# Attention and gated MLP in one kernel: fewer warming products, the softmax constant and the gate in other instructions, a new step order

## The chip, the cores and the metric

One core of a Trainium2 chip runs the whole program. The metric is device time in microseconds (us); the runs of the kernel before have a median of 676.97 us (three runs, 676.08 to 677.22). Less is better. The engines are named as in the profile: PE is TensorE (PEld its weight loads), DVE is VectorE, ACT is ScalarE, POOL is GpSimd, SP is the queue that issues the transfers.

## The reference

Two computations follow each other. The first is causal attention over 4 batches, 8 heads, 576 positions and 64 features, mixed by a gate per head with a retrieval from a memory matrix:

```python
a = np.exp(scores - scores.max(-1, keepdims=True))
a /= a.sum(-1, keepdims=True) + 1e-09
local = np.matmul(a, v)
g = 1.0 / (1.0 + np.exp(-beta))[None, :, None, None]
x = g * mem_out + (1 - g) * local
```

The second takes x as 2304 tokens of 512 features and computes ((x @ w_a) * (x @ w_b)) @ w_out with 1536 hidden features. The inputs k and z_prev are drawn eight times as wide as the others. Weights come as 64-bit floats, all else as 32-bit.

## The kernel before, in words

Work is cut into 16 **pairs** of heads (4 batches of 4 pairs). For each pair, steps with short names do this: `TK`, `TQ`, `Tq` transpose k, q and the last 64 rows on TensorE; `th*` and `tl*` split the results into a high and a low part (ScalarE and VectorE); `b_*` and `S_*` compute the mask and the scores, three products for each because of the split; `m*` takes the row minimum of the negated scores (line 574); `e*` is the exponential on ScalarE (line 585), which also writes each row's sum; `r_` makes the row factor on VectorE (lines 593 and 596); `n0` to `n4` multiply the five tiles of P by it on GpSimd (line 604), nine instructions for a pair, one for each row tile of 128 and head, with 128 to 512 columns, and one with 576 for the last rows of both heads; `G*` transposes P, `h*` and `l*` split that again, and `V*` multiplies by v (line 704), which `v_h` and `v_l` have split on GpSimd. `st_` stores the result to memory. `L*`, `D*` and `E*` are loads on SP's queue. Between these stand the memory retrieval (`ma` to `py`), the conversion of the MLP's weights (`mag` to `lo`), and from about 200 us on the MLP itself (lines 909 to 956), whose columns fill the rest of the time on TensorE.

The order is written out by hand. `HEAD` names every step for the first pairs. `LOOP` has two lists, each run through once for every loop position, with a lag behind each name that says how many pairs it runs behind; `SPAN` gives positions 3 to 8 to the first list and 9 to 13 to the second. `TAIL` names every step for the last pairs and the start of the MLP. `schedule` (line 114) yields the steps, and every engine takes its own instructions strictly in that order. `BANKS` gives each step that writes PSUM its bank.

In the row factor, the tile `sum` holds nine sums for each of 128 partitions. The step adds 1e-9 and multiplies by `over_ungate`, which is 1 + exp(beta), and so 1 over the share (1 - g), in one instruction, then takes the reciprocal:

```python
nc.vector.scalar_tensor_tensor(
    out=r, in0=r, scalar=1e-9, in1=over_ungate[:, j, :], op0=ALU.add, op1=ALU.mult
)
nc.vector.reciprocal(out=r, in_=r)
```

The scaling takes that factor as its first per-partition operand and the constant 1.0 as its second. `gates` (line 720) fills `over_ungate` once. `warm` (line 383) issues products of a tile of zeros on TensorE, whose results nobody reads: 17 and 12 of them, next to each other, at the very start while the first loads are on their way. `zi` (line 750) fills that tile with zeros.

Of the kernel before, what the change touches and what calls it, by code (L numbers as in the profile page):

```python
# [1283 lines left out]
```

## Time and profile before

| what | us |
|---|---|
| median of the runs | 676.97 |
| the profiled execution | 676.11 |
| its span, first to last instruction | 674.3 |
| TensorE busy in it | 660.1 |
| VectorE busy | 440.0 |
| ScalarE busy | 317.2 |
| GpSimd busy | 236.8 |

Busy time is counted over the whole span, though the first 206 us hold the attention, in which four engines work at once, and the rest the MLP, in which TensorE works almost alone. The busy time of TensorE contains each product's way through the array, so short waits between products don't show in it. A chain of waits is followed back from the last instruction to what released each one. A timeline row with a count merges instructions that follow one another.

### The profile page before, as it was taken

Reading aid. Unit: us, or ns where it says so; the run is one execution under the profiler, and the core shown is the slowest. Engines: PE = TensorE matmul, PEld = TensorE weight load, DVE = VectorE, ACT = ScalarE, POOL = GpSimd, SP = SyncE. Lnnn points to the kernel's source line nnn. Section 1 sums busy time; section 2 is a strip of 40 time slices with the busy share of each in tenths; the row PEclk is TensorE's granted clock in tenths of the full one; section 3 lists DMA queues with packets and bytes.
Section 4 is the critical chain, followed back from the end, with each engine's and each line's share of the span. In section 5 each row is a group of like instructions: output and inputs, shape, how many; then the busy total and the mean of one; then the engine's idle time right before and its main releaser. Section 6 shows DMA issues by size and latency. Waiting matters only on the chain.

```text
span 674.3 us, 11381 instructions
## 1 busy us (share of the span) xinstructions
PE 660.1 (98%) x4125; PEld 609.8 (90%) x4125; DVE 440.0 (65%) x901; ACT 317.2 (47%) x765; POOL 236.8 (35%) x354
## 2 busy tenths in 40 slices
...
GB/s 171 194 179 167 158 97 197 112 180 143 255 152 96 225 150 162 170 112 71 41 104 122 13 59 39 1 90 36 29 36 6 112 36 1 0 48 1 0 1 47
DMA packets 124663, 64.24 MB, mean 95 GB/s; under 512 B 97856, under 2 KB 116288, under 8 KB 124608
## 3 DMA queue, kind: packets, MB, share of 16 engines
...
q14 instruction: 23, 0.19, 0.1%
...
## 4 chain that ended last, share of the span: by engine, by line
PE 79%; DVE 15%; POOL 3%; ACT 2%; issue 1%; ACTq 0%; DVEq 0%; POOLq 0%
PE pp L909 43%; PE o L946 22%; DVE nm L574 4%; PE pt L187 4%; DVE PT L191 4%; PE pw L704 4%; PE pt L535 3%; POOL P L604 1%; PE m L1108 1%; DVE f L191 1%; PE pw L535 1%; PE pt L387 1%; DVE f L193 1%; DVE sum L593 1%; PE pt L909 1%
## 5 line engine op out<-in xcount | busy, mean ns | idle before, releaser
L909 PE MATMUL pp<-xh,wh 128*128 128x384 f32 x568 | 191.5, 337 | 1.8 <-ACT x L921 0.9
L909 PE MATMUL pp<-xh,wl 128*128 128x384 f32 x568 | 191.1, 336 | 0.0
L909 PE MATMUL pp<-xl,wh 128*128 128x384 f32 x568 | 190.4, 335 | 0.0
L924 DVE TENSOR_TENSOR x<-pp,x 128x384 f32<-128x384 f32 x71 | 39.4, 555 | 132.9 <-ACT x L921 121.7
L909 PEld LDWEIGHTS pp<-xh,wh 128*128 128x128 f32 x568 | 106.7, 188 | 5.7 <-ACT x L921 1.6
L909 PEld LDWEIGHTS pp<-xl,wh 128*128 128x128 f32 x568 | 106.7, 188 | 2.9
L909 PEld LDWEIGHTS pp<-xh,wl 128*128 128x128 f32 x568 | 106.6, 188 | 0.0
L921 ACT ACTIVATE x<-pp 128x384 f32<-128x384 f32 x71 | 34.6, 488 | 149.3 <-PE pp L909 134.4
L1100 POOL TENSOR_TENSOR xx<-xx 128x384 f32<-128x384 f32 x16 | 16.7, 1049 | 199.1 <-DMA xx<-xs 198.9
L946 PE MATMUL o<-wh,hl 128*128 128x512 f32 x216 | 85.5, 396 | 0.0
L946 PE MATMUL o<-wl,hh 128*128 128x512 f32 x216 | 85.0, 393 | 0.0
L946 PE MATMUL o<-wh,hh 128*128 128x512 f32 x216 | 84.9, 393 | 0.0
L604 POOL TENSOR_SCALAR P<-P,sum 128x128 f32<-128x128 f32 (+3 forms) x144 | 81.4, 585 | 7.0 <-DVE sum L596 7.0
L585 ACT ACTIVATE P<-pt,nm 128x128 f32<-128x128 f32 (+3 forms) x128 | 67.1, 532 | 11.3 <-DVE nm L574 10.2
L191 DVE TENSOR_TENSOR PT<-pt,PT 128x512 fp32r<-128x512 f32 (+2 forms) x112 | 61.7, 587 | 9.0 <-ACT PT L659 6.7
L704 PE MATMUL pw<-PT,vh 128*128 128x320 f32 (+4 forms) x416 | 62.0, 293 | 3.0 <-POOL P L604 1.1
L704 PEld LDWEIGHTS pw<-PT,vh 128*128 128x128 f32 x416 | 57.3, 189 | 6.0 <-POOL PT L191 1.6
L928 ACT ACTIVATE hh<-x 128x384 fp32r<-128x384 f32 x72 | 37.6, 523 | 50.7 <-DVE x L924 42.1
L191 DVE TENSOR_TENSOR hl<-x,hh 128x384 fp32r<-128x384 f32 x71 | 42.0, 591 | 27.8 <-ACT hh L928 27.6
L574 DVE TENSOR_REDUCE nm<-pt 128x1 f32<-128x128 f32 (+3 forms) x128 | 55.6, 479 | 5.3 <-PE pt L535 5.0
L187 PE MATMUL pt<-ident,P 128*128 128x128 f32 (+1 forms) x400 | 52.3, 276 | 2.0 <-POOL P L604 0.9
L659 ACT ACTIVATE PT<-pt 128x512 fp32r<-128x512 f32 (+2 forms) x112 | 52.1, 527 | 2.6 <-PE pw L704 2.0
...
## 6 DMA issues: line engine op xcount, KB each, us to landing
...
```

What stands on the lines that cost most here:

```text
L187: nc.tensor.transpose(out, x, ident[0:x.shape[0], 0:x.shape[0]])
L191: eng.tensor_tensor(out=lo, in0=x, in1=hi, op=ALU.subtract)
L574: nc.vector.tensor_reduce(out=s["nm"][:, c:c + 1], in_=src, axis=AX.X, op=ALU.min)
L585: nc.scalar.activation(out=s["P", i][:, h, :], in_=src, func=AF.Exp, scale=-1.0, bias=s["nm"][:, c:c + 1], accum_out=s["sum"][:, c:c + 1],)
L604: nc.gpsimd.tensor_scalar(out=pr[:, h, :], in0=pr[:, h, :], scalar1=r[:, c:c + 1], scalar2=1.0, op0=ALU.mult, op1=ALU.mult,)
L659: nc.scalar.activation(out=dst, in_=src, func=AF.Copy)
L704: nc.tensor.matmul(pv[:, a:hi], lhsT=w, rhs=x, start=(n == 0), stop=(n == len(ops) - 1))
L909: nc.tensor.matmul(pp, lhsT=w[:, w0:w0 + P], rhs=x[:, kk, :], start=(c == 0), stop=(c == 3 * KK - 1),)
L921: nc.scalar.activation(out=x, in_=ps[1], func=AF.Copy)
L924: nc.vector.tensor_tensor(out=h[0], in0=ps[0], in1=h[0], op=ALU.mult)
L928: nc.scalar.activation(out=h[1], in_=h[0], func=AF.Copy)
L946: nc.tensor.matmul(po[t, m], lhsT=hx[:, m * P:(m + 1) * P], rhs=w[:, w0:w0 + DM], start=(f == 0 and n == 0), stop=(f == NFT - 1 and n == 2),)
```

## The change

The single call of the warming step asks for 14 products where two calls asked for 17 and 12. The row sums get a tile of their own, two of them in turn: each sum is the first of a pair of columns whose second holds 1e-9, filled once in `zi`. `r_` adds up the pairs with one reduction and takes the reciprocal, without the gate. `gates` takes a reciprocal more, so that `ungate` holds (1 - g), and the scaling on GpSimd multiplies by it as its second per-partition operand. All four lists of steps and banks are new; the steps themselves, their engines and their number are the same but for the warming. The lists of `BANKS` and `TAIL` are left out here.

```diff
--- before.py
+++ after.py
@@ -19,95 +19,95 @@
 
 
 HEAD = """
-Dk.0 id.0 zi.0 ib.0 wm.17 wm.12 TK.0 Dq.0 Dk.1 TQ.0 zq.0 zq.1 thK.0 thQ.0 mk.0 Ek.1 TK.1 thK.1 b_2.0
-tlK.0 tlQ.0 S_2.0 m2A.0 Eq.0 e2A.0 b_3.0 Ek.0 S_3.0 tlK.1 m3A.0 sq.0 Dq.1 Lv.0 Tq.0 be.0 thq.0 Tq.1
-tlq.0 S_4.0 Lk.2 thq.1 m2B.0 tlq.1 TQ.1 e3A.0 e2B.0 b_.0 Lt.2 Lt.3 b_2.1 thQ.1 m3B.0 S_.0 m4.0 tlQ.1
-e3B.0 ms.0 mA.0 Lv.1 e4.0 mB.0 S_2.1 b_3.1 S_3.1 m2B.1 S_4.1 ga.0 m3A.1 eA.0 eB.0 v_h.0 TK.2 r_.0
-e2B.1 b_.1 Lk.3 v_l.0 e3A.1 thK.2 m2A.1 e2A.1 m3B.1 tlK.2 S_.1 ma.2 n0.0 mB.1 Tq.2 n4.0 thq.2 n1.0
-G0.0 n2.0 mb.2 G1.0 e3B.1 tlq.2 G5.0 G4.0 Lk.4 h0.0 TQ.2 h1.0 w_0.0 eB.1 thQ.2 G2B.0 mu.2 m4.1 h5.0
-l1.0 h4.0 G2A.0 n3.0 l0.0 h2B.0 G3B.0 mA.1 l5.0 eA.1 tlQ.2 l2B.0 l4.0 h2A.0 Lv.2 l2A.0 v_h.1 h3B.0
-l3B.0 G3A.0
+id.0 Dk.0 zi.0 ib.0 Dq.0 wm.14 TK.0 mk.0 Dk.1 Dq.1 Ek.0 b_2.0 thK.0 TQ.0 zq.0 Eq.0 zq.1 TK.1 thQ.0
+thK.1 tlK.0 tlQ.0 S_2.0 be.0 b_3.0 TQ.1 Ek.1 Lv.0 S_3.0 m2B.0 tlK.1 ms.0 thQ.1 b_.0 m2A.0 m3B.0
+e2B.0 sq.0 S_.0 tlQ.1 e2A.0 Tq.0 Lk.2 m3A.0 Tq.1 e3B.0 thq.0 thq.1 mB.0 tlq.0 e3A.0 mA.0 tlq.1 Lt.2
+ga.0 S_4.0 v_h.0 b_3.1 b_2.1 m4.0 v_l.0 eA.0 Lv.1 S_2.1 S_3.1 b_.1 eB.0 S_.1 m2A.1 TK.2 m3B.1 e4.0
+Lv.2 r_.0 TQ.2 e2A.1 mA.1 n4.0 G4.0 e3B.1 m2B.1 n0.0 S_4.1 eA.1 thK.2 n1.0 thQ.2 ma.2 h4.0 G0.0 Lk.3
+mB.1 n2.0 eB.1 m3A.1 G5.0 e2B.1 h0.0 G2B.0 G2A.0 tlK.2 Tq.2 G1.0 tlQ.2 h5.0 mb.2 m4.1 v_h.1 h2B.0
+n3.0 G3B.0 l4.0 h2A.0 w_0.0 thq.2 l0.0 mu.2 h1.0 l2B.0 l5.0 G3A.0 l2A.0 e3A.1 tlq.2 h3B.0 l1.0 Lt.3
+Lk.4 l3B.0
 """
 BANKS = """
...
 """
 LOOP = """
-H1:2 hh:4 pd:2 pe:3 shift1:3 TQ:0 py:4 h3A:3 me:3 clamp1:3 l3A:3 mx:3 e4:2 LM:2 b_3:1 thQ:0 px:4
-S_3:1 TK:0 cx:3 m3A:1 ma:0 r_:2 lo0:2 H0:3 Lp:1 mc:1 V1A:3 e3A:1 b_:1 V2A:3 Lt:-1 v_l:2 pb:2 thK:0
-tlQ:0 mb:0 pf:3 b_2:1 S_2:1 S_:1 xA:3 m3B:1 tlK:0 high1:3 m2B:1 n2:2 st_:4 n0:2 hl:4 V1B:3 Tq:0
-high2:3 clamp2:3 e3B:1 e2B:1 mA:1 pc:2 m2A:1 hi0:2 shift0:2 n4:2 eA:1 thq:0 md:1 low0:2 V2B:3 mag2:3
-e2A:1 high0:2 tlq:0 G5:2 xB:3 n1:2 mag0:1 G2B:2 h5:2 n3:2 lo1:4 low1:3 mu:0 G2A:2 sm:3 h2B:2 G0:2
-G1:2 mB:1 h0:2 l5:2 v_h:1 S_4:1 h2A:2 Lv:0 w_0:2 sq:-1 hi1:4 l2B:2 l2A:2 pa:1 h1:2 l1:2 shift2:3
-eB:1 m4:1 G4:2 h4:2 low2:3 l0:2 Lk:-2 G3B:2 clamp0:2 l4:2 h3B:2 mag1:2 G3A:2 l3B:2
+clamp0:2 clamp2:3 shift0:2 low2:3 TQ:0 hh:4 h3A:3 lo1:4 e4:2 Lt:-1 b_3:1 me:3 mc:1 ma:0 thQ:0 S_3:1
+l3A:3 clamp1:3 hi1:4 low1:3 pb:2 H1:2 pd:2 m3A:1 TK:0 v_l:2 V1A:3 V2A:3 pf:3 b_:1 b_2:1 Lp:1 LM:2
+r_:2 S_2:1 low0:2 mb:0 e3A:1 S_:1 thK:0 sq:-1 n4:2 V1B:3 tlQ:0 n2:2 m3B:1 Tq:0 xA:3 n0:2 mag0:1
+tlK:0 e3B:1 m2B:1 V2B:3 pe:3 m2A:1 mB:1 high2:3 mA:1 G0:2 e2B:1 md:1 e2A:1 n1:2 thq:0 G5:2 H0:3
+tlq:0 eB:1 lo0:2 shift2:3 mx:3 high0:2 xB:3 h5:2 py:4 n3:2 mu:0 G2A:2 G2B:2 h2A:2 G1:2 v_h:1 Lv:0
+S_4:1 h0:2 l5:2 G4:2 h2B:2 w_0:2 l2A:2 h1:2 hi0:2 eA:1 l2B:2 sm:3 st_:4 shift1:3 l1:2 l0:2 mag2:3
+hl:4 G3B:2 high1:3 m4:1 h4:2 pa:1 pc:2 cx:3 Lk:-2 h3B:2 mag1:2 l4:2 l3B:2 px:4 G3A:2
 /
-mc ma v_l mag0 b_3 Lk mag1 px h3A S_3 mu e4 pe TK l3A TQ V1A mag2 m3A pb pf r_ V2A st_ b_ b_2 shift2
-H0 S_2 pc S_ thK n1 H1 Tq V1B thQ high0 e3A n2 n4 tlQ xA clamp0 V2B G5 m3B high1 mx clamp2 mb G2B
-m2B G2A lo0 py e3B m2A G1 S_4 low1 e2B e2A thq n0 low0 LM mB G0 mA n3 eA xB tlq lo1 Lp tlK h5 l5 h2B
-pd sq l2B v_h me shift0 hi1 cx h2A hi0 G4 h1 eB Lv l2A G3B l1 h4 h0 G3A m4 Lt l4 sm clamp1 hl h3B hh
-w_0 low2 l0 shift1 l3B md high2 pa
+lo1 hh high1 px md v_l sq h3A b_3 me S_3 pe l3A e4 r_ TK TQ pb V1A high0 hi1 n1 V2A b_ b_2 shift1
+m3A thQ S_2 n2 n0 S_ Tq V1B mag0 V2B e3A thK n4 low2 pf pc tlQ xA mag2 G5 m3B G0 low0 mu G2B clamp2
+m2B Lk e3B G2A e2B m2A mc thq n3 G1 S_4 e2A py H0 mA eA xB h5 pd clamp0 v_h tlK h2B mB tlq ma shift0
+l5 low1 shift2 h0 h2A clamp1 w_0 h1 cx l2B G4 eB Lp G3B h4 high2 l2A Lt lo0 hi0 sm LM Lv l1 st_ h3B
+mx pa m4 l4 hl l0 mb mag1 l3B G3A H1
 """
 SPAN = (3, 9, 14)
 TAIL = """
...
 """
 
 
@@ -179,7 +179,8 @@
     ident = const.tile([P, P], F32, name="ident")
 
     over_gate = const.tile([P, H], F32, name="over_gate")
-    over_ungate = const.tile([P, NP, NTL], F32, name="over_ungate")
+    ungate = const.tile([P, NP, NTL], F32, name="ungate")
+    sums = [const.tile([P, NTL, 2], F32, name=f"sums{i}") for i in range(2)]
 
     over_gate_2 = const.tile([P, NP], F32, name="over_gate_2")
 
@@ -576,23 +577,20 @@
 
         @steps(*PARTS)
         def e(s, b, j, part):
-            if "sum" not in s:
-                s["sum"] = p2.tile([P, NTL], F32, tag="sum", name="sum")
+            s["sums"] = sums[j % 2]
             for i, h, c, src in scores(s, part):
                 if ("P", i) not in s:
                     shape = [P, 2 if i < NF else 1, src.shape[1]]
                     s["P", i] = p2.tile(shape, F32, tag=f"P{i}", name=f"P{i}")
                 nc.scalar.activation(
                     out=s["P", i][:, h, :], in_=src, func=AF.Exp, scale=-1.0,
-                    bias=s["nm"][:, c:c + 1], accum_out=s["sum"][:, c:c + 1],
+                    bias=s["nm"][:, c:c + 1], accum_out=s["sums"][:, c, 0:1],
                 )
 
         @steps("")
         def r_(s, b, j, part):
-            r = s["sum"]
-            nc.vector.scalar_tensor_tensor(
-                out=r, in0=r, scalar=1e-9, in1=over_ungate[:, j, :], op0=ALU.add, op1=ALU.mult
-            )
+            r = s["sum"] = p2.tile([P, NTL], F32, tag="sum", name="sum")
+            nc.vector.reduce_sum(out=r, in_=s["sums"], axis=AX.X)
             nc.vector.reciprocal(out=r, in_=r)
 
         @steps(*(str(i) for i in range(NF + 1)))
@@ -602,8 +600,8 @@
             for h in range(pr.shape[1]):
                 c = 2 * i + h
                 nc.gpsimd.tensor_scalar(
-                    out=pr[:, h, :], in0=pr[:, h, :], scalar1=r[:, c:c + 1], scalar2=1.0,
-                    op0=ALU.mult, op1=ALU.mult,
+                    out=pr[:, h, :], in0=pr[:, h, :], scalar1=r[:, c:c + 1],
+                    scalar2=ungate[:, j, c:c + 1], op0=ALU.mult, op1=ALU.mult,
                 )
 
 
@@ -722,13 +720,14 @@
             for t, sign in ((u, 1.0), (over_gate, -1.0)):
                 nc.scalar.activation(out=t, in_=beta_t, func=AF.Exp, scale=sign)
                 nc.vector.tensor_scalar(out=t, in0=t, scalar1=1.0, scalar2=None, op0=ALU.add)
+            nc.vector.reciprocal(out=u, in_=u)
             u2 = u.rearrange("p (j e) -> p j e", e=2)
             for e in range(2):
                 r = slice(64 * e, 64 * e + 64)
                 nc.vector.tensor_copy(
-                    over_ungate[:, :, e:2 * NF:2], u2[:, :, e:e + 1].to_broadcast([P, NP, NF])
-                )
-                nc.vector.tensor_copy(over_ungate[r, :, NTL - 1], u2[r, :, e])
+                    ungate[:, :, e:2 * NF:2], u2[:, :, e:e + 1].to_broadcast([P, NP, NF])
+                )
+                nc.vector.tensor_copy(ungate[r, :, NTL - 1], u2[r, :, e])
 
         beta_t = p1.tile([P, H], F32, name="beta_t")
         mask = p2_e.tile([P, P], BF16, name="mask", bufs=1)
@@ -747,7 +746,10 @@
                 nc.vector.tensor_copy(mask_t[r], mask_f[r, r])
 
         step |= {
-            "zi": lambda _: nc.vector.memset(idle.bitcast(F32), 0.0),
+            "zi": lambda _: (
+                nc.vector.memset(idle.bitcast(F32), 0.0),
+                [nc.vector.memset(t[:, :, 1], 1e-9) for t in sums],
+            ),
             "zq": blank,
             "id": lambda _: make_identity(nc, ident),
             "ib": lambda _: nc.vector.tensor_copy(ident_b, ident),
```

## Rows read from the trace of the kernel before

**Rows 1.** Busy time by stages: us, then PE, PEld, DVE, ACT, POOL; clock, DMA.
```profile
28.00:88.00 60.00, 58.78 (x510) 52.57 (x510) 59.13 (x132) 56.14 (x163) 57.84 (x90) 1.00 0.61 158
...
100.00:155.00 55.00, 55.00 (x491) 50.88 (x489) 47.58 (x106) 50.18 (x150) 51.59 (x86) 1.00 0.65 167
155.00:206.00 51.00, 48.05 (x404) 43.38 (x403) 44.12 (x87) 42.89 (x116) 48.83 (x75) 1.00 0.53 168
206.00:300.00 94.00, 92.68 (x494) 86.77 (x493) 82.38 (x111) 47.19 (x70) 20.74 (x21) 1.00 0.49 164
```

**Rows 2.** Chain of waits by lines: 28 to 100 us, then 155 to 206 us.
```profile
by line: DVE nm L574 26.3%; DVE PT L191 25.7%; PE pt L187 6.0%; DVE f L191 5.8%; DVE ph L272 5.1%; PE pw L704 4.6%; DVE f L193 4.5%; DVE sum L593 4.3%; DVE rn L282 4.2%; PE pt L535 3.8%; DVE ph L269 3.0%; DVE sum L596 1.8%; issue 1.6%; DVE 
...
by line: PE pw L704 12.3%; POOL P L604 12.2%; DVE PT L191 8.8%; POOL vh L191 6.5%; PE pt L187 6.3%; PE pt L535 6.2%; PE pt L909 4.0%; POOL xl L191 3.8%; POOL xx L323 3.8%; issue 3.0%; POOL PT L191 2.9%; DVE wt L880 2.7%; DVE wt L873 2.7%; D
```

**Rows 3.** Timeline, 0 to 26 us: start, us, engine, line, operation, count, idle before.
```profile
1.19 5.64 PE L387 MATMUL pt<-idle 128*128 128x256 f32 x29 [1.19 <-DVE idle L750]
...
6.66 0.60 PE L187 MATMUL pt<-ident,kr 128*128 128x128 f32 x4
...
7.10 0.60 PE L187 MATMUL pt<-ident,qr 128*128 128x128 f32 x4
...
7.93 0.69 DVE L191 TENSOR_TENSOR f<-pt,f 128x512 fp32r<-128x512 f32 x1 [4.63 <-ACT f L511]
```

**Rows 4.** Warming products by stretch: us, PE, PEld, granted clock, DMA share, GB/s.
```profile
3.00:4.00 1.00, 1.00 (x7) 1.00 (x6) 1.00 1.02 230
```

**Rows 5.** First loads of k, then of q: issue (ns, first and last start) and landing.
```profile
L425 SPq DMA_DIRECT2D kr<-in_k_dram x2: 442/467/492, 0.7 to 1.2; - x2
DMA to landing us min/median/max: 2.3/2.6/2.9
...
L425 SPq DMA_DIRECT2D qr<-in_q_dram x2: 499/503/507, 1.8 to 2.3; - x2
DMA to landing us min/median/max: 2.9/2.9/2.9
```

**Rows 6.** Timeline of POOL, 8 to 60 us: three groups of row scalings.
```profile
18.09 4.18 POOL L604 TENSOR_SCALAR P<-P,sum 128x128 f32<-128x128 f32 x7 [3.06 <-DVE sum L596]
...
39.92 4.97 POOL L604 TENSOR_SCALAR P<-P,sum 128x384 f32<-128x384 f32 x9 [0.66 <-DVE sum L596]
...
51.69 4.98 POOL L604 TENSOR_SCALAR P<-P,sum 128x384 f32<-128x384 f32 x9 [0.38 <-DVE sum L596]
```

**Rows 7.** Lines 593 and 596, whole span: ns least, median, most; first and last start.
```profile
L593 DVE SCALAR_TENSOR_TENSOR sum<-sum,over_ungate x16: 158/276/1625, 17.5 to 191.9; 128x9 f32<-128x9 f32 x16
...
L596 DVE RECIPROCAL sum<-sum x16: 215/216/217, 17.7 to 193.1; 128x9 f32<-128x9 f32 x16
```

**Rows 8.** Timelines of VectorE and GpSimd, 60 to 90 us.
```profile
86.22 1.62 DVE L593 SCALAR_TENSOR_TENSOR sum<-sum,over_ungate 128x9 f32<-128x9 f32 x1
...
86.53 1.29 POOL L191 TENSOR_TENSOR vh<-vr,vh 128x512 fp32r<-128x512 f32 x1
```

**Rows 9.** Pieces of the chain, start and us: to 20 us, then 28 to 100.
```profile
9.27 1.55 PE pt L535 x8
...
62.76 0.36 DVE sum L593
...
86.30 1.55 DVE sum L593
```

**Rows 10.** VectorE's groups by form, whole span: count, busy us, mean ns, idle before.
```profile
L574 DVE TENSOR_REDUCE nm<-pt 128x1 f32<-128x512 f32 x32 | 21.7, 680 | 0.2
...
L574 DVE TENSOR_REDUCE nm<-pt 128x1 f32<-128x128 f32 x32 | 8.9, 279 | 1.7 <-PE pt L535 1.6
```

**Rows 11.** GpSimd by form: one operand (111 to 115.9 us), then none (whole span).
```profile
L604 POOL TENSOR_SCALAR P<-P,sum 128x512 f32<-128x512 f32 x2 | 1.4, 688 | 0.0
...
L604 POOL TENSOR_SCALAR P<-P,sum 128x128 f32<-128x128 f32 x2 | 0.7, 367 | 0.0
...
L451 POOL TENSOR_SCALAR qdiag<-qdiag 128x512 f32<-128x512 f32 x4 | 2.5, 615 | 5.1 <-DMA qdiag<-in_q_dram 5.1
...
L476 POOL TENSOR_SCALAR vh<-vt 128x128 fp32r<-128x128 f32 x16 | 4.7, 296 | 0.7 <-DMA vt<-in_v_dram 0.7
```

More of the change, by code (lines that the diff above doesn't have):

```diff
@@ new lines @@
+pe.12 h4.12 G2B.12 l0.12 l3A.12 v_l.13 m3B.14 e3B.14 r_.13 pd.13 V1A.12 h2B.12 Tq.14 l4.12 TQ.15
+pf.12 m3A.14 h3B.12 V2A.12 n0.13 thq.14 b_.14 l3B.12 thQ.15 n2.13 tlq.14 n1.13 st_.11 e3A.14 xA.12
+pa.13 b_2.14 l2B.12 pb.13 tlQ.15 S_.14 S_2.14 TK.15 n3.13 pc.13 mA.14 V1B.12 eA.14 Tq.15 G0.13
+thK.15 m2A.14 n4.13 m2B.14 V2B.12 e2B.14 G3A.13 thq.15 G4.13 tlK.15 v_h.14 G5.13 S_4.14 h0.13 mB.14
+xB.12 Lp.14 pe.13 tlq.15 v_l.14 w_0.13 h3A.13 h5.13 h4.13 l3A.13 l5.13 G2A.13 eB.14 G1.13 m4.14
+e2A.14 h2A.13 pf.13 G3B.13 h1.13 px.12 b_3.15 l0.13 S_3.15 l4.13 pa.14 l2A.13 e4.14 h3B.13 px.13
@@ new lines @@
+l1.13 pb.14 r_.14 m3B.15 G2B.13 V1A.13 pc.14 py.12 h2B.13 e3B.15 V2A.13 xA.13 b_.15 b_2.15 S_.15
+S_2.15 l3B.13 V1B.13 m3A.15 l2B.13 n4.14 mB.15 e3A.15 V2B.13 m2A.15 m2B.15 n3.14 eB.15 G3B.14 e2A.15
+n0.14 e2B.15 G4.14 xB.13 pd.14 h3B.14 n2.14 mA.15 G5.14 S_4.15 l3B.14 eA.15 h5.14 G0.14 n1.14 m4.15
+l5.14 h4.14 v_h.15 v_l.15 l4.14 G1.14 G2A.14 to.0 h0.14 e4.15 G3A.14 h3A.14 w_0.14 l0.14 h1.14
+h2A.14 r_.15 n0.15 l3A.14 l1.14 n2.15 l2A.14 G2B.14 mag0.15 pe.14 h2B.14 V1A.14 V2A.14 clamp0.15
+l2B.14 st_.13 G2A.15 mag1.15 shift0.15 st_.12 n4.15 n1.15 G2B.15 V1B.14 high0.15 V2B.14 G4.15 G5.15
@@ new lines @@
+Khi.3 umx.1 Kshift.4 Klo.3 uA.2 Kload.8 uhh.1 Kload.9 uhl.1 Kmag.5 Kclamp.5 Khigh.4 Klow.4 Kshift.5
+Kload.10 uB.2 ucx.2 umx.2 uA.3 Khi.4 uhh.2 Kmag.6 Klo.4 uhl.2 Khigh.5 uB.3 Kclamp.6 Klow.5 Kshift.6
+Khigh.6 ucx.3 umx.3 uo.2 uA.4 Klow.6 Khi.5 uB.4 uhh.3 uo.1 Klo.5 uA.5 Khi.6 Kmag.7 uhl.3 uB.5 Klo.6
+ucx.4 Kclamp.7 Kmag.8 uo.3 Kshift.7 Kload.11 umx.4 Kclamp.8 Khigh.7 Klow.7 uhh.4 Kshift.8 uhl.4
+Khi.7 uA.6 Khigh.8 Klo.7 uB.6 Kload.13 ucx.5 Kmag.9 Klow.8 umx.5 Khi.8 uhh.5 Kload.12 uo.4 Kclamp.9
@@ new lines @@
+Kload.14 Kshift.9 Klo.8 Khigh.9 Klow.9 Kmag.10 ucx.6 Kload.16 Kclamp.10 uhl.5 Khi.9 Kshift.10 uA.7
+umx.6 uB.7 Klo.9 Kmag.11 uo.5 uA.8 Khigh.10 uhh.6 uhl.6 Klow.10 Kclamp.11 Kshift.11 Khi.10 Klo.10
+Kload.15 ucx.7 umx.7 uB.8 Kmag.12 uhh.7 ucx.8 Khigh.11 Klow.11 uo.6 Kclamp.12 uhl.7 Kshift.12 Khi.11
+Khigh.12 uA.9 Klow.12 Khi.12 Kmag.13 Klo.11 uB.9 umx.8 uhh.8 Kclamp.13 uo.7 uhl.8 Kshift.13 uA.10
+Klo.12 uB.10 Khigh.13 Kmag.14 Klow.13 ucx.9 umx.9 Kclamp.14 uhh.9 uo.8 Khi.13 Kmag.15 Kshift.14
+ucx.10 Khigh.14 Kload.18 uA.11 Klow.14 uhl.9 Klo.13 Khi.14 Kclamp.15 umx.10 Kshift.15 Klo.14 Kmag.16
@@ new lines @@
+Khigh.15 uB.11 Kload.17 uo.9 uhh.10 Klow.15 Kclamp.16 Kshift.16 Kload.20 ucx.11 uA.12 uB.12 uhl.10
+Khigh.16 Kload.22 umx.11 Kload.19 uo.10 uhh.11 uA.13 Kload.21 Klow.16 Khi.15 Khi.16 uhl.11 uB.13
+uo.11 Kmag.17 Kmag.18 Klo.15 Klo.16 ucx.12 uA.14 Kclamp.17 Kshift.17 Kclamp.18 umx.12 Kshift.18
+Khigh.18 uB.14 uhh.12 Klow.18 Khigh.17 Khi.18 uhl.12 Klo.18 ucx.13 Klow.17 Kmag.20 umx.13 Kclamp.20
+uo.12 Kload.23 Khi.17 Kmag.19 Kshift.20 Klo.17 Khigh.20 uhh.13 uhl.13 Kclamp.19 Kshift.19 ucx.14
+Klow.20 umx.14 Khi.20 Khigh.19 Kmag.22 Klow.19 Klo.20 uA.15 uhh.14 uo.13 uB.15 Khi.19 Kmag.21 ucx.15
```

93 lines of the change are left out of this document (32 added, 61 removed).

## The prediction

> **What bounds the kernel now.** I read the busy time by stages first [rows 1], then the chain of waits by lines [rows 2]. From 206 us on TensorE is busy with 1.3 us of gaps in 94: no operation of that stage changes, and what is won or lost before it moves it as a whole. So the first 206 us decide. Up to 28 us the pipeline fills, and the row of warming products is the longest piece of the chain. From 28 to 88 us VectorE is busy 59.13 of 60 us, and the chain is mostly its instructions; GpSimd stands close behind with 57.84. From 100 to 155 us TensorE has no gap, VectorE 7.4 us spare and GpSimd 3.4. From 155 to 206 us the chain passes between TensorE, GpSimd and VectorE, and GpSimd is busy 48.83 of 51. Then I followed the two lines that change, the row-sum step on VectorE and the scaling of P on GpSimd, into the timeline and the chain.
>
> **Warming products.** Today 29 products run from 1.19 us, and the first transposes of k follow them directly at 6.66, those of q at 7.10 [rows 3]. They stand behind the products alone, not behind their data. The products take 5.64 us, 0.19 us from one to the next. [...] The second half of the first k is issued at 1.24 and takes up to 2.9 us: it is in at 4.1, so its transposes can start 2.4 us sooner. The first q, second half issued at 2.3, is in at 5.2: 1.9 us sooner than used now [rows 5]. [...] I take **-1.2 us**. Bounds: 0, if another part of the filling pipeline holds the scores, and -2.4. On SP's queue the second pair's q now goes ahead of the tails of k and q, beta ahead of the second batch's k tail, and the first v some half a microsecond later. GpSimd, which splits that v, idles 3.06 us before 18.09 for the row sums [rows 6], and that covers it; without that cover it would cost its half microsecond.
>
> **Setup.** The two fills with 1e-9 come on VectorE at about 1 us, in the 4.63 us for which it idles before its first use of k [rows 3]: nothing. The reciprocal of the gate sits among the gate steps, ahead of the first row sums, where VectorE is full: **+0.2 us**, by the 216 ns of the other small reciprocal [rows 7].
>
> **Row sums.** Sixteen steps. The old instruction takes 158 ns at the least, 276 in the median, 1625 at the most, on nine columns; the reciprocal behind it always 215 to 217 [rows 7]. So it is not arithmetic. The old step reads two operands in SBUF, and where it is long it ends with a two-input instruction of GpSimd: one runs from 86.53 to 87.82, and the step from 86.22 to 87.84 [rows 8]. In the VectorE stage it is on the chain six times: four times with 0.36 us, as at 62.76, once with 0.09 and once with 1.55 [rows 9], 3.1 us together. The new sum has one input and should be free of this. Reductions of 512 and 128 columns take 680 and 279 ns [rows 10], 1.04 ns a column and 146 ns fixed, so 18 columns take 165 ns, much as the unhindered old step, some 0.1 us on the chain: six make 0.6, and 2.5 us go. GpSimd allows less: its group of nine starts at 39.92 and again at 51.69, of which 0.38 us is waiting for the row sums [rows 6]; 11.77 can shrink to 11.39 at most, plus what the new scaling adds. I take **-2.2 us**. Bounds: 0, if GpSimd sets the pace, and -2.5. From 100 to 155 us TensorE covers the step: nothing. From 155 to 206 us one long wait of about a microsecond may be on the chain, out of what is left of the sixteen; I take **-0.9**, bounds 0 and -1.5.
>
> **Scaling on GpSimd.** 144 instructions get a second per-partition operand where a constant stood. The trace has no such form. It has one operand and none: 688 against 615 ns at 512 columns, 367 against 296 at 128 [rows 11]. The first operand costs 72 ns. The upper bound for the second is the same again, 144 x 72 = 10.4 us of GpSimd; the lower is nothing, if the form that fetches one fetches both. No row excludes either. The nearest row would say 72, but it measures the step from constants to operands, not from one to two, so I take less, 20 ns: 0.18 us for a group of nine. Up to 88 us this is already in the -2.2; from 100 to 155 GpSimd's 3.4 idle us take it in; from 155 to 206, four groups, **+0.7**.
>
> [...]
>
> **New order.** Steps and engines stay, the sequence on each engine changes, its transfers included. TensorE idles 2.95 us from 155 to 206 and 1.3 up to 300 [rows 1], so an order may win some 1.5 us there, and an operand that comes late may lose as much. I take 0, with 1.5 either way.
>
> **Sum.** -1.2 + 0.2 - 2.2 - 0.9 + 0.7 = -3.4 us against the profiled execution's 676.11 (span 674.3): 672.7. The median of the runs, 676.97, lies 0.86 higher: 673.6.
>
> **Rivals.** *First: GpSimd becomes the bound, and it is slower.* With 72 ns a group of nine grows by 0.65 us. In the VectorE stage GpSimd's period becomes 12.04 for 11.77, +1.35 us in five periods, about what the one long stall gives back: 0. From 100 to 155 us its idle 3.4 us lie unevenly before the groups; of five times 0.65 I count a third, +1.1. From 155 to 206, four times 0.65 less some 0.9 of its idle time: +1.7. With -1.2 and +0.2 that is +1.8: 678.8, and up to 681 with a bad order. It decides from about 42 ns on, where 11.39 us and nine times the price reach 11.77. For it: GpSimd is 96% busy, and the first operand has this price. Against: both may come in one fetch.
>
> [...]
>
> *Third: the change frees nothing that matters.* TensorE is busy 58.78 of 60 us in the VectorE stage, so VectorE may win idle time alone; with the start's -1.0 and +0.5 for the order, 676.5.
>
> **How the numbers follow.** Forecast 0.50, first rival 0.27, second 0.10, third 0.13. The likeliest's own range is 671 to 675.5. The range for 8 in 10 leaves about a tenth on either side: 670.5 (start at -2.4, a better order) and 680.0, inside the first rival. A measurement tells about 0.2%, 1.35 us: faster ends at 675.6, slower begins at 678.3. The forecast gives faster 0.46, the same 0.04; the second and third give 0.08, 0.14 and 0.01; the first gives the same 0.05 and slower 0.22. Together faster 0.54, same 0.23, slower 0.23.
>
> **What would show it.** Right: the first transposes of k at 4.2 to 4.5 us, the first scores a microsecond sooner; the sum at 150 to 200 ns with no long ones and hardly on the chain; the scaling at 512 columns below 715 ns; about 11.5 us from group to group in the VectorE stage. Wrong: 512 columns at 750 ns or more and GpSimd without idle time from 28 us on (first rival); early transposes that take double their time (second); a sum without long waits, and yet the TensorE stage at 206 us reached no sooner than the start alone explains (third).

## The result, and the profile after

The changed kernel takes 682.0 us (median of six runs, 681.35 to 683.71) where the kernel before takes 676.49 in the same call: ratio 1.0088, 95% interval 1.0071 to 1.0106. It is 0.9% slower, above the whole predicted range, in the direction of the first rival.

| | before | after |
|---|---|---|
| the profiled execution, us | 676.11 | 683.25 |
| its span | 674.3 | 681.5 |
| TensorE busy | 660.1 | 659.6 |
| VectorE busy | 440.0 | 445.7 |
| ScalarE busy | 317.2 | 317.4 |
| GpSimd busy | 236.8 | 246.3 |

GpSimd has 9.5 us more to do, VectorE 5.7, TensorE no more than before. The busy time by stages, in the columns of [rows 1], with the stretch between the first two stages as a row of its own; the last row is that stretch in the kernel before:

```profile
28.00:88.00 60.00, 57.49 (x496) 50.33 (x495) 59.11 (x127) 53.70 (x157) 59.06 (x86) 1.00 0.62 148
88.00:100.00 12.00, 9.39 (x74) 8.79 (x74) 11.20 (x22) 7.93 (x26) 11.76 (x19) 0.88 0.57 149
100.00:155.00 55.00, 54.73 (x491) 50.66 (x489) 47.38 (x104) 49.53 (x142) 51.79 (x83) 0.99 0.60 149
155.00:206.00 51.00, 46.41 (x394) 41.38 (x392) 41.17 (x86) 41.92 (x120) 49.08 (x73) 1.00 0.63 191
206.00:300.00 94.00, 91.19 (x495) 86.14 (x495) 79.03 (x107) 47.67 (x73) 25.17 (x27) 0.98 0.42 138
...
88.00:100.00 12.00, 11.31 (x103) 10.49 (x103) 11.57 (x27) 10.55 (x33) 10.62 (x20) 1.00 0.52 117
```

In the VectorE stage GpSimd is now as full as VectorE, 59.06 and 59.11 of 60 us, and TensorE does 496 products there instead of 510. From 88 to 100 us TensorE idles 2.6 us, for 0.7 before, and its granted clock averages 0.88, for 1.00. The chain of waits by lines, from 28 to 100 us, 100 to 155 and 155 to 206, names the engine that the end now waits for; the last line is the kernel before, from 100 to 155 us:

```profile
by line: DVE nm L575 29.6%; DVE PT L192 25.7%; DVE ph L273 9.3%; DVE f L192 6.2%; DVE rn L284 6.1%; DVE rn L283 5.0%; DVE f L194 4.1%; DVE ph L270 2.6%; PE pt L188 2.4%; PE pw L536 2.3%; PE pt L536 1.5%; DVE sum L594 1.5%; DVE rn L287 1.5%;
...
by line: POOL P L602 42.0%; POOL vh L192 10.8%; DMA vr<-in_v_dram 7.1%; issue 6.6%; POOL xx L324 5.3%; POOL PT L192 5.2%; POOL vh L477 4.7%; POOL xl L192 3.6%; PE pt L188 2.9%; POOL xh L345 2.6%; POOL PT L669 2.1%; POOL ph L291 1.8%; ACT P 
...
by line: POOL P L602 34.0%; DMA xx<-xs 12.0%; DMA xs<-xo 9.0%; POOL xx L324 5.7%; issue 5.2%; POOL vh L192 4.4%; ACT P L585 4.4%; POOL xl L192 4.0%; POOL vh L477 3.4%; POOL PT L192 2.6%; PE pt L188 1.7%; POOL PT L669 1.5%; POOL md L192 1.5%
...
by line: PE pt L187 31.5%; PE pw L704 23.2%; PE pt L535 22.9%; PE pw L535 6.7%; PE pt L333 5.3%; DVE nm L574 3.8%; ACT P L585 2.9%; ACT PT L659 2.5%; ACT xo L713 1.0%; issue 0.2%; ACTq L585 0.1%
```

From 100 us on the scaling on GpSimd (line 602) is the largest link, 42 and 34%; before, GpSimd was not in the chain from 100 to 155 us, and the scaling had 12.2% behind that [rows 2]. Before 100 us two steps of VectorE have grown. Line 273 (272 before), which joins the two parts of phi, has 9.3%, against 5.1 in [rows 2]; line 284 (283 before), which adds 1e-6 to the retrieval's denominator and multiplies it by the gate, has 6.1%, and is not among the lines that [rows 2] shows.

The scaling itself, by form, in a stretch in which nothing disturbs it (114 to 121 us), as in [rows 11]: count, busy us, mean ns.

```profile
L602 POOL TENSOR_SCALAR P<-P,sum,ungate 128x512 f32<-128x512 f32 x2 | 1.5, 774 | 0.0
L602 POOL TENSOR_SCALAR P<-P,sum,ungate 128x384 f32<-128x384 f32 x2 | 1.3, 668 | 0.0
L602 POOL TENSOR_SCALAR P<-P,sum,ungate 128x256 f32<-128x256 f32 x2 | 1.1, 558 | 0.2 <-DVE sum L594 0.2
L602 POOL TENSOR_SCALAR P<-P,sum,ungate 128x128 f32<-128x128 f32 x2 | 0.9, 454 | 0.0
```

At 512 columns it is 774 ns for 688, at 128 columns 454 for 367: 86 and 87 ns more, so the width hardly matters. A group of nine takes 5.57 us where it took 4.80.

Three lines of VectorE (ns least, median, most): the new row sum, and the two remaining steps with two operands in SBUF.

```profile
L593 DVE TENSOR_REDUCE sum<-sums x16: 162/164/174, 15.8 to 198.6; 128x9 f32<-128x18 f32 x16
...
L273 DVE SCALAR_TENSOR_TENSOR ph<-qr,ph x6: 852/1557/1565, 21.9 to 82.0; 128x512 f32<-128x512 f32 x6
...
L284 DVE SCALAR_TENSOR_TENSOR rn<-rn,over_gate x6: 292/314/2765, 32.0 to 93.3; 128x8 f32<-128x8 f32 x6
```

The row sum is flat, where [rows 7] had up to 1625 ns. But line 273 has a median of 1557 ns (816 before, on line 272), and one execution of line 284, on eight columns, took 2765 (332 at the most before, on line 283). The long steps are gone from the row sum, and there are new ones at the two others.

The start, in the columns of [rows 3]:

```profile
1.19 3.36 PE L388 MATMUL pt<-idle 128*128 128x256 f32 x14 [1.19 <-DVE sums L751]
4.34 0.92 PE L188 MATMUL pt<-ident,kr 128*128 128x128 f32 x4
...
5.33 0.63 PE L188 MATMUL pt<-ident,qr 128*128 128x128 f32 x4
6.53 0.63 PE L188 MATMUL pt<-ident,kr 128*128 128x128 f32 x4 [0.57 <-DMA kr<-in_k_dram]
```

The transposes of k begin at 4.34 us for 6.66. The first group of scalings begins at 16.41 for 18.09 [rows 6]. Where the 7 us then come from is read off the starts of the groups:

| start of a group of scalings, us | before | after | difference |
|---|---|---|---|
| first pair | 18.09 | 16.41 | -1.7 |
| second | 28.43 | 28.33 | -0.1 |
| sixth | 75.24 | 76.67 | +1.4 |
| seventh | 88.20 | 89.92 | +1.7 |
| eighth | 99.18 | 103.47 | +4.3 |
| twelfth | 147.30 | 151.46 | +4.2 |
| sixteenth | 193.39 | 201.07 | +7.7 |

So the lead of the start is gone by the second group, the VectorE stage loses 1.8 us, one place near 95 us loses 2.6, and the stretch from 151 to 201 us 3.5. In that stretch the chain also holds 10.7 us of transfers of x (12.0 and 9.0%, above), where it had none before, and GpSimd waits once, 1.43 us, for a load of v, where it waited 0.85 before. The place near 95 us, in timelines of VectorE, GpSimd and TensorE:

```profile
93.32 2.77 DVE L284 SCALAR_TENSOR_TENSOR rn<-rn,over_gate 128x8 f32<-128x8 f32 x1
...
89.92 5.56 POOL L602 TENSOR_SCALAR P<-P,sum,ungate 128x576 f32<-128x576 f32 x9
95.46 0.61 POOL L477 TENSOR_SCALAR vh<-vr 128x512 fp32r<-128x512 f32 x1
...
96.69 0.67 PE L188 MATMUL pt<-ident,P 128*128 128x128 f32 x4 [2.44 <-DVE f L192]
```

The step on eight columns starts inside a group of scalings and ends at 96.09, just after the next GpSimd instruction. VectorE does nothing else meanwhile, and TensorE waits 2.44 us for what is queued behind that step. The granted clock of the next stretches (third column from the right):

```profile
96.00:98.00 2.00, 1.31 (x8) 1.32 (x9) 1.82 (x6) 0.60 (x2) 1.83 (x5) 0.79 0.87 198
98.00:100.00 2.00, 2.00 (x11) 1.99 (x10) 1.45 (x2) 0.90 (x5) 1.92 (x3) 0.50 0.30 64
100.00:102.00 2.00, 2.00 (x17) 1.84 (x17) 1.32 (x2) 1.59 (x3) 1.48 (x3) 0.86 0.00 0
...
206.00:208.00 2.00, 2.00 (x12) 2.00 (x12) 0.69 (x2) 0.00 (x0) 2.00 (x4) 0.59 0.00 0
208.00:210.00 2.00, 2.00 (x12) 1.96 (x12) 0.95 (x2) 1.44 (x2) 1.52 (x3) 0.55 0.00 0
```

0.50 is the lowest clock in these rows: after its gap TensorE runs slowly for some 3 us (11 products from 98 to 100 us, for 21 before), and again at 206 us (12 products from 206 to 208, for 15), after a stretch (200 to 206) in which it is busy 3.42 us of 6. Summed over these five stretches the clock falls short by 2 x (0.21 + 0.50 + 0.14 + 0.41 + 0.45) = 3.4 us, which bounds what the clock can have cost in this execution. Before, these stretches had 1.00.

### The profile page after: what moved, and what is told of

Read it like the earlier page. It is cut to its first block, busy times and chain, and to the rows that moved or that the text cites. A ratio compares the mean times of both kernels' runs of the same rounds, so it can differ in the third digit from the quotient of the medians.

```text
span 681.5 us, 11334 instructions
## 1 busy us (share of the span) xinstructions
PE 659.6 (97%) x4110; PEld 609.6 (89%) x4110; DVE 445.7 (65%) x904; ACT 317.4 (47%) x765; POOL 246.3 (36%) x354
## 4 chain that ended last, share of the span: by engine, by line
PE 66%; DVE 13%; POOL 12%; DMA 3%; ACT 2%; issue 2%; SPq 1%; POOLq 0%; ACTq 0%
PE pp L911 41%; PE o L948 20%; POOL P L602 7%; DVE nm L575 4%; DVE PT L192 3%; PE pt L188 1%; PE m L1110 1%; POOL vh L192 1%; PE pw L702 1%; DVE ph L273 1%; DMA xx<-xs 1%; POOL xx L324 1%; DVE f L192 1%; DMA wr<-in_moe_w_out_dram 1%; POOL vh L477 1%
## 5 line engine op out<-in xcount | busy, mean ns | idle before, releaser
L602 POOL TENSOR_SCALAR P<-P,sum,ungate 128x256 f32<-128x256 f32 (+4 forms) x144 | 93.2, 665 | 3.5 <-DVE sum L594 3.5
L192 DVE TENSOR_TENSOR PT<-pt,PT 128x512 fp32r<-128x512 f32 (+2 forms) x112 | 62.5, 589 | 11.8 <-ACT PT L657 7.1
L188 PE MATMUL pt<-ident,P 128*128 128x128 f32 (+1 forms) x400 | 56.9, 283 | 7.1 <-POOL P L602 3.1
L575 DVE TENSOR_REDUCE nm<-pt 128x1 f32<-128x512 f32 (+3 forms) x128 | 55.3, 479 | 6.1 <-PE pt L536 6.0
```

The source lines that it names most:

```text
L188: nc.tensor.transpose(out, x, ident[0:x.shape[0], 0:x.shape[0]])
L192: eng.tensor_tensor(out=lo, in0=x, in1=hi, op=ALU.subtract)
L575: nc.vector.tensor_reduce(out=s["nm"][:, c:c + 1], in_=src, axis=AX.X, op=ALU.min)
L602: nc.gpsimd.tensor_scalar(out=pr[:, h, :], in0=pr[:, h, :], scalar1=r[:, c:c + 1], scalar2=ungate[:, j, c:c + 1], op0=ALU.mult, op1=ALU.mult,)
```

## The experiments

**Theory:** the second per-partition operand makes every scaling some 85 ns longer; the time goes into GpSimd's own queue and into lines 273 and 284, steps of VectorE with two operands in SBUF, which wait beside GpSimd's instructions as the old row sum did [rows 8]. **Rival:** the new order loses the time, whatever the instructions. A second question is whether the row sum and the shorter start are worth what the sum gave them.

**Changed instructions in the old order** (29 products, old lists). The diff against the kernel before:

```diff
-            nc.vector.scalar_tensor_tensor(
-                out=r, in0=r, scalar=1e-9, in1=over_ungate[:, j, :], op0=ALU.add, op1=ALU.mult
-            )
+            nc.vector.reduce_sum(out=r, in_=s["sums"], axis=AX.X)
...
-                    out=pr[:, h, :], in0=pr[:, h, :], scalar1=r[:, c:c + 1], scalar2=1.0,
-                    op0=ALU.mult, op1=ALU.mult,
+                    out=pr[:, h, :], in0=pr[:, h, :], scalar1=r[:, c:c + 1],
+                    scalar2=ungate[:, j, c:c + 1], op0=ALU.mult, op1=ALU.mult,
...
```

> The changed instructions (pair sums, gate as second operand on GpSimd) in the step order of before, with its 29 products. Theory 'price' (the second operand's 85 ns, 16 groups of nine grown from 4.80 to 5.57 us in the changed kernel's trace, make GpSimd the bound): some 4 us of the 12 us reach the end, 679 to 682 us. Theory 'order' (the new sequence is what loses): the freed waits of the row sums are won, 674 to 676 us.

Measured: 681.25 us (680.67 to 685.45), ratio 1.0084 (1.0061 to 1.0106). The instructions alone, in the old order and with the old products, lose about as much as the whole change. Timelines of GpSimd and VectorE in it:

```profile
54.66 5.72 POOL L602 TENSOR_SCALAR P<-P,sum,ungate 128x384 f32<-128x384 f32 x9 [0.73 <-DVE sum L594]
60.35 0.62 POOL L477 TENSOR_SCALAR vh<-vr 128x512 fp32r<-128x512 f32 x1
60.94 0.82 POOL L477 TENSOR_SCALAR vh<-vt 128x128 fp32r<-128x128 f32 x1
...
67.59 1.48 POOL L602 TENSOR_SCALAR P<-P,sum,ungate 128x384 f32<-128x384 f32 x2 [0.75 <-DMA zr<-in_z_prev_dram]
...
58.88 0.78 DVE L284 SCALAR_TENSOR_TENSOR rn<-rn,over_gate 128x8 f32<-128x8 f32 x1
...
60.03 1.57 DVE L273 SCALAR_TENSOR_TENSOR ph<-qr,ph 128x512 f32<-128x512 f32 x1
```

From one group to the next it is 12.93 us, for 11.77 before, and yet GpSimd idles 0.73 to 0.75 in each: here it is not the bound. Line 284 takes 0.78 us, and line 273, which starts 0.35 us before the group ends, 1.57. Both lie on the path of VectorE, which sets the period.

**New order and 14 products, old instructions.** The diff is the lists of the recorded change and `wm.14` alone:

```diff
-Dk.0 id.0 zi.0 ib.0 wm.17 wm.12 TK.0 Dq.0 Dk.1 TQ.0 zq.0 zq.1 thK.0 thQ.0 mk.0 Ek.1 TK.1 thK.1 b_2.0
+id.0 Dk.0 zi.0 ib.0 Dq.0 wm.14 TK.0 mk.0 Dk.1 Dq.1 Ek.0 b_2.0 thK.0 TQ.0 zq.0 Eq.0 zq.1 TK.1 thQ.0
...
```

> The new step order with its 14 products, and the instructions of before (1e-9 and gate in one two-input step on VectorE, one operand on GpSimd). 'Price': the start's 1.7 us are kept, 674 to 676 us. 'Order': the loss is here, 679 to 682 us, with long two-input steps on VectorE while GpSimd runs its groups, and the granted clock below 1 near 96 us.

Measured: 677.42 us (12 runs), ratio 1.002 (1.0009 to 1.0031). The order and the shorter start together lose 0.2%, between what the two theories forecast. The shorter start hides part of what the order loses; the pairs of runs at the end of this section hold the products equal. Already with the old scaling this order makes line 283 wait: 1192 ns in the median and 1521 at the most, for 177 and 332 before.

**The gate on ScalarE, in the new order and in the old.** The gate goes from the scaling to ScalarE's copy of the output, which takes a per-partition scale; the second operand of the scaling is a constant again, and the row sum stays the changed one. Against the changed kernel (the second also with the old lists and 29 products):

```diff
-                    scalar2=ungate[:, j, c:c + 1], op0=ALU.mult, op1=ALU.mult,
+                    scalar2=1.0, op0=ALU.mult, op1=ALU.mult,
...
-            nc.scalar.activation(out=s["xo"][:, h, :], in_=s["V", h], func=AF.Copy)
+            c = 2 * j + h
+            nc.scalar.activation(
+                out=s["xo"][:, h, :], in_=s["V", h], func=AF.Copy, scale=ungate[:, c:c + 1]
+            )
```

> The changed kernel, but the gate is applied by ScalarE as the scale of its copy of the output (32 copies), so that the scaling on GpSimd has one operand and the constant again. 'Price': groups of nine fall back to 4.80 us, 674 to 676.5 us. 'Order': 679 to 682 us, with the groups at 4.80 us all the same.

> The order and the 29 products of before, the row sums by pairs, the gate as the scale of ScalarE's copies. Both theories: the waits of the row sums behind GpSimd go (VectorE's step at 164 ns each time) and GpSimd pays nothing, 673 to 675.5 us. If it is not faster than before, those waits were not worth anything in the first place.

Measured: new order 677.3 us, ratio 1.0015 (1.0005 to 1.0026), above the 676.5 at most that was expected of 'price'; old order 674.24, ratio 0.9971 (0.9957 to 0.9985). Against the same kernels with the operand, 682.0 and 681.25, the second operand costs 4.7 and 7.0 us. The old order without it, GpSimd's groups and two lines of VectorE:

```profile
51.22 4.99 POOL L602 TENSOR_SCALAR P<-P,sum 128x384 f32<-128x384 f32 x9
62.73 4.99 POOL L602 TENSOR_SCALAR P<-P,sum 128x384 f32<-128x384 f32 x9
...
L273 DVE SCALAR_TENSOR_TENSOR ph<-qr,ph x6: 805/818/822, 20.8 to 79.0; 128x512 f32<-128x512 f32 x6
...
L284 DVE SCALAR_TENSOR_TENSOR rn<-rn,over_gate x6: 183/190/457, 32.3 to 89.9; 128x8 f32<-128x8 f32 x6
```

The period is 11.51 us, the groups no longer wait for the row sums, and lines 273 and 284 are short again. Of the 1.42 us that the operand adds to a period, 9 x 82 ns = 0.73 are the scalings themselves; the 1.57 - 0.82 and 0.78 - 0.19 us of the two steps make 1.3, and it is these that lie on VectorE's path.

**The same two kernels without the two steps.** Lines 273 and 284 are left out of both (so phi lacks its maximum part, and the retrieval's denominator the 1e-6 and the gate):

```diff
-            nc.vector.scalar_tensor_tensor(
-                out=ph, in0=qr, scalar=0.0, in1=ph, op0=ALU.max, op1=ALU.add
-            )
+            pass
...
-            nc.vector.scalar_tensor_tensor(
-                out=rn2, in0=rn2, scalar=1e-6, in1=over_gate, op0=ALU.add, op1=ALU.mult
-            )
```

> ops_only (681.25 us) without the two two-input steps of the memory part on VectorE that had become long, lines 273 and 284 (the larger-than-zero part of phi, the 1e-6 and the gate of the retrieval are left out). Theory 'price through VectorE' (GpSimd's longer groups reach the end because these two steps wait for them; GpSimd itself has time left): distance from group to group falls from 12.93 to about 11.4 us between 40 and 95 us if VectorE alone counts, but not under GpSimd's own 12.1; in all 676 to 678 us. Rival 'GpSimd alone': 12.1 to 12.9 us, 679 to 681 us.

> The same two steps left out of old_order_gate_scalar (674.24 us), as the counterpart of ops_free: there they are not long (0.82 and 0.19 us), GpSimd is busy all the time, so little goes: 672.5 to 674 us, 11.3 to 11.5 us from group to group.

Measured: with the operand 676.28 us, ratio 1.0003 (0.9993 to 1.0012); with the gate on ScalarE 673.87, ratio 0.9967 (0.9953 to 0.9981). Leaving the steps out is worth 5.0 us with the operand (681.25 to 676.28) and 0.4 without it (674.24 to 673.87). So of the 7.0 us that the operand costs in the old order, 4.6 go when these two steps are left out, and 2.4 remain. That those 2.4 are GpSimd's longer queue is likely, but no run shows it.

**The second operand alone.** The kernel before with a column of ones for the constant, everything else unchanged:

```diff
-                    out=pr[:, h, :], in0=pr[:, h, :], scalar1=r[:, c:c + 1], scalar2=1.0,
+                    out=pr[:, h, :], in0=pr[:, h, :], scalar1=r[:, c:c + 1],
+                    scalar2=ones[:, j, c:c + 1],
```

> The kernel before with one edit: the second operand of the 144 scalings is a column of ones in the place of the constant 1.0; sums, order and products as before. 'Price' theory: all that ops_only lost, and without the gain of the freed row sums, 680 to 684 us, groups of nine at 5.57 us or longer. Rival (the second operand alone is harmless, the loss in ops_only needs the pair sums): 675.5 to 678 us.

Measured: 687.27 us (686.94 to 690.09), ratio 1.0179 (1.016 to 1.0198): 11.6 us for nothing but the operand, more than the 684 us at most that were expected. By form, from 42 to 56 us:

```profile
L605 POOL TENSOR_SCALAR P<-P,sum,ones 128x512 f32<-128x512 f32 x2 | 1.5, 768 | 0.0
L605 POOL TENSOR_SCALAR P<-P,sum,ones 128x128 f32<-128x128 f32 x2 | 0.9, 449 | 0.0
```

80 and 82 ns more than [rows 11]. From group to group it is again 12.94 us. The price is larger than the 7.0 us above. Up to 94 us the two kernels with the operand keep together (groups at 94.82 and 94.17); after that this one falls back, with the old row sum at 1.56 us before the fifteenth group and 1.07 before the last (at 191 and 202 us), where the changed one takes 0.16. By the last group that is 2.6 us; the span is 7.5 us longer, so most of it comes later and wasn't traced. Between these two kernels the changed row sum is worth 6.0 us, against 2.1 with the short scalings; no run takes this apart further.

**The changed kernel without line 284.** The diff is the second part of the one above, against the changed kernel (the retrieval's denominator lacks the 1e-6 and the gate).

> The changed kernel without the two-input step at line 284 (six times, 8 columns; 1e-6 and the gate of the retrieval are left out). It stood for 2.77 us at 93.32 behind GpSimd's scalings, then TensorE idled and its granted clock fell. 'Lock' theory: those 2.6 us, the clock's 1.5 and some 0.2 us of each other one go, 677 to 679 us, granted clock 1.00 at 96 to 102 us. Rival (GpSimd sets the pace there in any case, VectorE only fills its time): 680.5 to 682 us.

Measured: 679.94 us, ratio 1.0061 (1.0044 to 1.0078): about 2 us of the 5.5 hang on this one small step, between what the two theories forecast. Granted clock after the place where it stalled, and at 206 us:

```profile
96.00:98.00 2.00, 2.00 (x20) 1.84 (x19) 2.00 (x4) 2.00 (x8) 1.83 (x5) 1.00 1.06 254
98.00:100.00 2.00, 2.00 (x18) 1.64 (x16) 1.97 (x6) 1.68 (x6) 1.92 (x3) 1.00 0.84 164
...
206.00:212.00 6.00, 5.09 (x34) 4.36 (x33) 5.55 (x9) 4.91 (x10) 5.92 (x7) 1.00 0.00 1
```

The clock stays at 1.00 where the gap is gone; the rest of the loss stays. How much of the 2 us is the gap and how much the clock this run doesn't separate; the profile of the changed kernel with 29 products, below, does.

**14 products in the old kernel, 29 in the changed one.**

```diff
-Dk.0 id.0 zi.0 ib.0 wm.17 wm.12 TK.0 Dq.0 Dk.1 TQ.0 zq.0 zq.1 thK.0 thQ.0 mk.0 Ek.1 TK.1 thK.1 b_2.0
+Dk.0 id.0 zi.0 ib.0 wm.14 TK.0 Dq.0 Dk.1 TQ.0 zq.0 zq.1 thK.0 thQ.0 mk.0 Ek.1 TK.1 thK.1 b_2.0
...
-id.0 Dk.0 zi.0 ib.0 Dq.0 wm.14 TK.0 mk.0 Dk.1 Dq.1 Ek.0 b_2.0 thK.0 TQ.0 zq.0 Eq.0 zq.1 TK.1 thQ.0
+id.0 Dk.0 zi.0 ib.0 Dq.0 wm.29 TK.0 mk.0 Dk.1 Dq.1 Ek.0 b_2.0 thK.0 TQ.0 zq.0 Eq.0 zq.1 TK.1 thQ.0
```

> The kernel before with 14 products in one call. 'Start' theory: a gain of about 1.2 us, 674.5 to 675.5 us. Rival (start hidden behind the loads or eaten by the lower clock): 676 to 677 us.

> The changed kernel with 29 products in its one call. If the start's gain reaches the end there too, 683 to 684 us. If GpSimd's longer groups take it in (the second group begins at 28.33 us against 28.43 before, though the first began 1.7 us sooner), 681.5 to 682.5 us.

Measured: the old kernel with 14 products 675.27 us, ratio 0.999 (0.9981 to 0.9999); the changed one with 29 products 684.76, ratio 1.0134 (1.0119 to 1.0149). Groups of the first of them:

```profile
17.06 4.20 POOL L604 TENSOR_SCALAR P<-P,sum 128x128 f32<-128x128 f32 x7 [1.91 <-DVE sum L596]
...
27.82 4.99 POOL L604 TENSOR_SCALAR P<-P,sum 128x384 f32<-128x384 f32 x9 [0.38 <-DVE sum L596]
39.92 5.00 POOL L604 TENSOR_SCALAR P<-P,sum 128x384 f32<-128x384 f32 x9 [0.91 <-DVE sum L596]
```

One microsecond ahead of [rows 6] at the first group, 0.6 at the second, nothing at the third, which waits longer for its row sum. In the old order the shorter start is worth 0.1%. In the changed order it is worth 684.76 - 682.0, about 2.8 us, and by the two ratios 3.1: more than was expected of it there. Why the same products weigh more in that order wasn't traced; only that the later start of 2.6 us at the first group (19.04 for 16.41) is still there at the sixth (79.32 for 76.67).

The profile with 29 products has the same stall, in timelines of VectorE and TensorE, and a different clock behind it:

```profile
95.96 2.76 DVE L284 SCALAR_TENSOR_TENSOR rn<-rn,over_gate 128x8 f32<-128x8 f32 x1
...
99.33 0.63 PE L188 MATMUL pt<-ident,P 128*128 128x128 f32 x4 [2.44 <-POOL PT L669]
...
100.00:102.00 2.00, 2.00 (x18) 2.00 (x18) 1.92 (x5) 2.00 (x7) 1.92 (x3) 1.00 0.60 128
```

TensorE waits 2.44 us in both, but here its clock stays at 1.00. From the seventh group to the eighth it is 11.94 us, for 13.55 with the lower clock and 11.58 without line 284 (101.91 - 90.33). So up to the eighth group the lower clock cost 1.6 us in the one execution, and the gap itself 0.4.

**Both useful parts together:** the old order, the changed row sum, the gate on ScalarE, 14 products.

```diff
+            nc.vector.reduce_sum(out=r, in_=s["sums"], axis=AX.X)
...
+                out=s["xo"][:, h, :], in_=s["V", h], func=AF.Copy, scale=ungate[:, c:c + 1]
...
-Dk.0 id.0 zi.0 ib.0 wm.17 wm.12 TK.0 Dq.0 Dk.1 TQ.0 zq.0 zq.1 thK.0 thQ.0 mk.0 Ek.1 TK.1 thK.1 b_2.0
+Dk.0 id.0 zi.0 ib.0 wm.14 TK.0 Dq.0 Dk.1 TQ.0 zq.0 zq.1 thK.0 thQ.0 mk.0 Ek.1 TK.1 thK.1 b_2.0
```

> old_order_gate_scalar (674.24 us) with 14 products in one call for 17 and 12. 'Start' theory: the first scores come a microsecond sooner and the VectorE stage behind them is shifted by that, 672.5 to 673.7 us. Rival: the pipeline's filling is held elsewhere, or TensorE stays at its lower level, 674 to 676 us.

Measured: 672.88 us (671.71 to 674.67), ratio 0.9956 (0.9938 to 0.9973), the fastest here: 0.4% below the kernel before. Two of its groups:

```profile
39.19 4.99 POOL L602 TENSOR_SCALAR P<-P,sum 128x384 f32<-128x384 f32 x9 [0.73 <-DVE sum L594]
...
190.30 7.73 POOL L602 TENSOR_SCALAR P<-P,sum 128x384 f32<-128x384 f32 x9 [0.42 <-DVE sum L594]
```

The last one begins at 190.30 us, against 190.82 with 29 products and 193.39 before: here half a microsecond of the shorter start is kept to the end.

**The order alone, by pairs of the runs above.** Three pairs have the same instructions and the same number of products and differ in the lists of steps and banks. By their ratios the new order costs 0.30% with the old instructions and 14 products (1.002 and 0.999), 0.50% with the changed ones and 29 (1.0134 and 1.0084), 0.59% with the gate on ScalarE and 14 (1.0015 and 0.9956): 2.0, 3.4 and 4.0 us, and in no pair do the intervals touch. Line 284 in the last pair, new order first, and then GpSimd's load of v in the new order:

```profile
L284 DVE SCALAR_TENSOR_TENSOR rn<-rn,over_gate x6: 168/1188/2104, 32.1 to 91.8; 128x8 f32<-128x8 f32 x6
...
L284 DVE SCALAR_TENSOR_TENSOR rn<-rn,over_gate x6: 192/194/459, 31.6 to 89.4; 128x8 f32<-128x8 f32 x6
...
179.41 0.62 POOL L477 TENSOR_SCALAR vh<-vr 128x512 fp32r<-128x512 f32 x1 [2.29 <-DMA vr<-in_v_dram]
```

So even with the short scalings the new order makes line 284 wait, and it makes a load of v come late: GpSimd waits 2.29 us for it here and 2.11 with the old instructions, for 0.85 before. What each of the two costs at the end wasn't tried.

## Why the prediction was wrong

**The first step that failed** is "Scaling on GpSimd", where the second operand was taken at 20 ns because the row of the first "measures the step from constants to operands, not from one to two". It costs 78 to 87 ns, more than the 72 of the first: above the upper bound that the sum had used. Where +0.7 us stood, the operand costs 4.7 us in the new order and 7.0 in the old. The argument against the first rival, "both may come in one fetch", finds no support in these numbers. Over the 144 scalings, 82 to 87 ns each make 11.8 to 12.5 us of GpSimd; what in the operand takes the time no run shows.

**The second step that failed** is "New order", taken as "0, with 1.5 either way". With equal instructions and products it costs 2.0 to 4.0 us. From the fastest kernel at 672.88 us, near the forecast of 673.6, the order leads to 677.3 and the operand from there to 682.0: each of the two carries about half of the miss on this way. On the other way, operand first, the shares are 7.0 and 3.4 us, and the shorter start then gives 2.8 back; what a part costs depends on which others are in. The profiles show two places for the loss of the order. One was not looked at: line 284 falls into GpSimd's groups. The other is the one that was named, an operand that comes late between 155 and 206 us, the load of v.

**The first rival** had the right place and sign: above its 42 ns it decides, the scaling at 512 columns passes its 750 ns, and GpSimd holds the chain from 100 us on. Put 83 ns for 72 into its own sum, and 678.8 becomes about 679.8; it allowed 681 with a bad order. For the old order and products, without the -1.2 of the start, the same sum gives 681.0, and 681.25 was measured, but that it comes so near is luck. In the old order VectorE stays the bound of its stage, and GpSimd idles there: from the second group to the seventh that kernel loses 4.3 us where the sum has 0.5, from the eighth to the sixteenth 1.8 where it has 3.3. Of the operand's 7.0 us there, 4.6 come through two steps of VectorE that the change doesn't touch and that longer scalings hold up. The prediction had read this mechanism off the row sum [rows 8], and line 272 stood in the chain with 5.1% [rows 2], but it priced the longer scaling on GpSimd alone. That lines 272 and 283 have two operands in SBUF too was left out; in the changed kernel they take up to 1565 and 2765 ns, for 819 and 332.

**Row sums: right in kind, two thirds of the size.** The new sum takes 164 ns where 165 were worked out, and no long one is left: 162 to 174 ns for the reduction, 158 to 1625 for the step it replaces. With the gate off GpSimd, the profiled execution gains 1.8 us from the first group to the one at 97.21 and 0.6 later, where -2.2 and -0.9 stood; over all runs 0.29%, 2.0 us (interval 1.0 to 2.9).

**Warming products: the early part right, the worth not.** The transposes of k came at 4.34 us, between the 4.2 and 4.5 forecast, but no run shows the 1.2 us that the sum took for the start, an estimate of the author's: in the old order 1.0 us of lead reached the first scaling. Then it was lost by 40 us, near the bound of 0: by the ratio 0.7 us stay in the old order, by the groups 0.5 in the fastest kernel. In the changed kernel it is worth 2.8 us, above the bound of 2.4, and that wasn't explained. The sum counted a lead at 9 us as one at the end, with a VectorE stage in between that sets its own pace. The sign named for the second rival, early transposes that take double their time, did not come: the four behind the products took 0.92 us, the next groups 0.63, for 0.60 before.

**Third rival: refuted.** Freed time of VectorE does reach the end, as the kernel with the gate on ScalarE shows.
